# Transposing B, C and y of the last two batches with VectorE and a trip through DRAM instead of TensorE, with the second part of the work order rewritten

## The chip, the cores and the metric

The kernel runs on one core of one Trainium2 chip. The metric is the device time of one execution in microseconds (us), as the median of several runs. Five engines work side by side on the core and wait for one another through semaphores: TensorE (PE in the profile; its weight loads have a row of their own, PEld), VectorE (DVE), ScalarE (ACT), GpSimd (POOL) and SyncE (SP). Each engine takes its instructions strictly in the order in which they were written. In this kernel every DMA is issued by SP.

## The reference

Two blocks follow one another. The first is a state-space scan (Mamba2 in chunks), the second a token mixer of low rank followed by a two-layer network on the channels.

```python
# x (4, 8, 768, 32), a (4, 8, 768), B and C (4, 8, 768, 16): batch, head, step, size
for c in range(seq // 32):                      # per batch and head
    cum = cumsum(log(clip(a_c)))
    L = exp(cum[:, None] - cum[None, :]) * causal
    y_intra = ((C_c @ B_c.T) * L) @ x_c
    y_inter = (C_c @ state) * exp(cum)[:, None]
    y_c = y_intra + y_inter
    state = exp(sum(la)) * state + sum_j(B_j x_j * exp(cum[-1] - cum_j))
x = y.transpose(0, 2, 1, 3).reshape(4, 768, 256)        # heads side by side
h = x.transpose(0, 2, 1) @ U @ V                        # U (768, 32), V (32, 768)
u = x + h.transpose(0, 2, 1)
out = u + relu(u @ w_ch1) @ w_ch2                       # 256 -> 1024 -> 256
```

All inputs and the output are float32 (the weights of the second block come as float64 and are taken apart on the chip).

## The kernel before

**The scan** works on pairs of 128-step blocks. There are 4 batches with 3 pairs each, so pairs 0 to 11; pairs 6 to 8 belong to batch 2 and pairs 9 to 11 to batch 3. The steps of one pair are small functions. `load` brings B, C and x from DRAM. `prep` multiplies B and C by their decays into a tile BC (VectorE, one instruction of 128x512 elements). `turning` transposes the four 128x128 blocks of BC on TensorE into PSUM, from where ScalarE copies them to the tile T and writes two scaled versions of the C half to the tile Cm. `gram` multiplies Cm and T (TensorE), `mask` applies causality (VectorE), `state` and `update` advance the state, `inter` and `intra` make y in PSUM, and `yout` (ScalarE) copies y to yT, a tile with the channels on the partitions. `ytokening` transposes a pair of yT blocks back on TensorE into PSUM and copies them to ytok, a tile with the steps on the partitions (mostly by ScalarE for batches 0 and 1, by VectorE for batches 2 and 3).

**The mixer** of a batch takes ytok of all three pairs. `project` (p) multiplies it by U in 24 instructions, eight for each pair, in the order of the pairs; its result is copied to pT by ScalarE. `mixed` (x) multiplies by V into four PSUM banks, `added` (a) adds the result to yT on VectorE in two halves of two additions each.

**The channel network** of a batch goes over three blocks of 256 steps. `split` (S) cuts the block into a near, a far and a combined part (one ScalarE and two VectorE instructions), so that float32 products can be made of three fast products. `first` (f, 8 matmuls), `second` (e, 4 matmuls and a ReLU on ScalarE) and `third` (h, two VectorE instructions of 128x512) make a quarter of the hidden layer; `piece` (d) makes four matmuls of the second weight matrix at a time, thirteen pieces to a block, the last of which transposes or writes out. For batches 1 and 2 and most of 3 the last piece is a VectorE transpose in 32x32 squares and four DMAs of 64 KB to the output (line 909). Blocks 0 and 1 of batch 0 are computed in plain float32 products (`plain`, U, and slower pieces).

**Order.** Nothing is scheduled by the compiler: the strings in PLANS list the steps as words, and every word emits its instructions at its place on all the engines that it uses. The letters are P prep, D decayed, T turned (TensorE transposes of one pair, half of them per word), g gram, m and M mask, s state, u update, i inter, n intra, y yout, t ytokens, L load, R refined (weights), and p x a S f e h d for the mixer and the network with a lag: `p-1` is the projection of batch 2 and `p-2` that of batch 3, while T3 to T8 and t3 to t8 are the words of pairs 6 to 11. The tiles of PSUM come in three tags: w with two banks, x and z with three banks each. `gram`, `intra` and `mixed` each take two banks of x and two of z; `first` and the pieces take one.

Lines that matter below: 497, 501 and 507 (`turning`: transposes, copy to T, writes to Cm), 714 and 728 (`ytokening`), 529 (`gram`), 684 (`intra`), 659 (`inter`), 748 (`project`), 760 (`mixed`), 791 (all products of the channel network), 195 (loads), 909 and 923 (outputs). VectorE instructions go through a helper and are all on line 169.

Of the kernel before, what the change touches and what calls it, by code (L numbers as in the profile page):

```python
# [14 lines left out]
WCOLS = 512  # L15
NWORDS = 12
PLAIN = 2
ROWS = 3
FOUR = 3

# [50 lines left out]
}  # L71


# [1 line left out]
def kernel(  # L75
# [410 lines left out]
    def turning(k, c=0, n=2, tag="w", engine=None, sooner=False):  # L486

        s = st[k]
        if c == 0:
            s["T"] = att.tile([P, 2, 2, P], FP32, tag="T", name="T", bufs=3)  # L490
            s["Cm"] = att.tile([P, 2, 2, P], FP32, tag="Cm", name="Cm", bufs=3)
        tp = bank(tag, 2, n, P)
        for i in range(2):
            for v in range(n):
                if i or v:
                    yield
                nc.tensor.transpose(out=tp[:, i, v],  # L497
                                    in_=s["BC"][:, i, c + v].rearrange("p h n -> p (h n)"),
                                    identity=ident)
        if sooner or not engine:  # L500
            nc.scalar.copy(out=s["T"][:, :, c:c + n], in_=tp)
        for i in range(2):
            if engine:
                engine.tensor_scalar(out=s["Cm"][:, i, c:c + n], in0=tp[:, 1],
                                     scalar1=slot[:, i, None], scalar2=None, op0=ALU.mult)
            else:
                nc.scalar.activation(s["Cm"][:, i, c:c + n], tp[:, 1], AF.Copy,
                                     scale=slot[:, i, None])
        if engine and not sooner:
            nc.scalar.copy(out=s["T"][:, :, c:c + n], in_=tp)  # L510
        yield

    def turn(*args):
# [457 lines left out]

    def turned(k):

        t = turns.setdefault(k, turning(k))
        for _ in range(2):
            next(t)

    def crossed(k):

# [2 lines left out]
    def ytokens_of(k, v):  # L982
# [3 lines left out]

    scans = dict(P=prep, D=decayed, T=turned, g=gram, s=state, m=lambda k: mask(k, (0, 1)),
                 M=lambda k: mask(k, (2, 3)), u=update, i=lambda k: inter(k, 0), n=intra,
                 j=crossed, y=yout, t=ytokens, L=load, Q=lambda k, c: prep(k, c, 1),
                 E=lambda k, c: decayed(k, c, 1), O=ytokens_of,  # L990
                 V=lambda k, c, v: turn(k, c, 1, "wx"[v // 2 % 2], vector if v % 2 else None, v > 3))
    whole = dict(c=convert, R=refined, A=lambda i: decays(every_batch, "w", [i]),
# [56 lines left out]
```

## Time and profile before

| | |
|---|---|
| median of 3 runs | 219.41 us (219.27 to 221.42) |
| the profiled execution | 219.55 us, of which 217.8 us from the first to the last instruction |
| mean granted TensorE clock | 0.992 |
| busy: PE, PEld, DVE, ACT | 205.9, 185.1, 168.3 and 125.0 us |
| instructions: PE, DVE, ACT | 3246, 349 and 287 |
| DMA by the kernel | 83,984 packets, 14.13 MB |

The table gives busy time per engine within the span. The times in the profile count from the first instruction. A group such as "PE w L714 x4" in the chain is four instructions of line 714 that write a tile with tag w: here the four transposes of one pair.

### The profile page before, as it was taken

How to read it: one execution, taken by the hardware profiler on the slowest of the kernel's cores; microseconds unless marked ns; L12 is line 12 of the kernel's file. 1: busy time of each engine (PE TensorE's matmuls, PEld its weight loads, DVE VectorE, ACT ScalarE, POOL GpSimd, SP SyncE). 2: the span in 40 equal slices, each digit the busy share in tenths (PEclk: the TensorE clock that was granted, in tenths of full speed). 3: DMA queues.
4: the chain of work that ended last, by engine and by line, in shares of the span. 5: the costliest groups of instructions: out<-in, count | busy, mean ns of one | idle time of the engine just before them, and what ended most of it. 6: DMA issues, size and time to landing. Idle time of an engine off the chain costs nothing.

```text
span 217.8 us, 7530 instructions
## 1 busy us (share of the span) xinstructions
PE 205.9 (95%) x3246; PEld 185.1 (85%) x3246; DVE 168.3 (77%) x349; ACT 125.0 (57%) x287; POOL 6.6 (3%) x22
## 2 busy tenths in 40 slices
PE   7778799999999999999999999979999999999994
PEld 5555586878879998999999988869999899999993
DVE  3398978998899998699858967847994597874871
ACT  3353749479969774368589513667563276635410
POOL 4132100000000000000000000000000000000000
PEclk9999969999999999999999999999999999999999
DMA  5996789986751017406600020330000000033234
GB/s 82 134 159 178 105 123 225 249 147 157 99 73 26 3 50 97 52 16 87 147 6 0 0 40 14 50 54 0 3 0 3 3 2 0 3 48 51 36 60 96
DMA packets 84016, 14.60 MB, mean 67 GB/s; under 512 B 80336, under 2 KB 82192, under 8 KB 83984
## 3 DMA queue, kind: packets, MB, share of 16 engines
q1 hardware_dynamic: 83984, 14.13, 37.0%
q8 instruction: 25, 0.41, 0.9%
q14 instruction: 7, 0.06, 0.1%
HBM read 10.98 MB, written 3.15 MB: 65 GB/s over the span
## 4 chain that ended last, share of the span: by engine, by line
PE 83%; DVE 6%; ACT 3%; SPq 2%; issue 2%; DMA 2%; POOL 1%; DVEq 0%
PE x L791 35%; PE z L791 28%; PE x L529 3%; SPq L195 2%; PE w L497 2%; PE w L748 2%; PE w L714 2%; DMA bc<-in_B_dram 2%; DVE words L169 2%; PE x L760 2%; PE x L684 1%; PE x L659 1%; PE w L564 1%; PE z L684 1%; DVE M L169 1%
## 5 line engine op out<-in xcount | busy, mean ns | idle before, releaser
L169 DVE SCALAR_TENSOR_TENSOR words<-words 128x512 fp32r<-128x512 f32 (+6 forms) x60 | 39.3, 667 | 4.3 <-PE x L791 1.4
L791 PE MATMUL x<-words,w 128*128 128x256 f32 x288 | 38.3, 280 | 0.0
L791 PEld LDWEIGHTS x<-words,w 128*128 128x128 f32 x288 | 34.9, 188 | 1.8 <-issue 1.7
L791 PE MATMUL z<-u,w 128*128 128x256 f32 x240 | 34.0, 280 | 1.3 <-issue 1.3
L791 PE MATMUL x<-u,w 128*128 128x256 f32 x240 | 34.0, 281 | 0.0
L791 PEld LDWEIGHTS z<-u,w 128*128 128x128 f32 x240 | 30.1, 188 | 1.6 <-issue 1.3
L791 PEld LDWEIGHTS x<-u,w 128*128 128x128 f32 x240 | 30.1, 188 | 0.6 <-issue 0.2
L796 ACT ACTIVATE z<-z 128x512 f32<-128x512 f32 (+1 forms) x24 | 13.9, 578 | 18.0 <-PE z L791 18.0
L796 ACT ACTIVATE x<-x 128x512 f32<-128x512 f32 (+1 forms) x27 | 15.4, 574 | 14.5 <-PE x L791 14.3
L169 DVE SCALAR_TENSOR_TENSOR words<-x,words 128x512 fp32r<-128x512 f32 x20 | 13.7, 685 | 10.7 <-ACT words L831 10.5
L791 PE MATMUL z<-words,w 128*128 128x256 f32 x144 | 19.3, 280 | 0.0
L791 PEld LDWEIGHTS z<-words,w 128*128 128x128 f32 x144 | 17.5, 188 | 0.4 <-issue 0.4
L831 ACT ACTIVATE words<-z 128x512 fp32r<-128x512 f32 x20 | 11.8, 601 | 6.1 <-PE x L791 4.3
L831 ACT ACTIVATE words<-x 128x512 fp32r<-128x512 f32 x20 | 11.8, 600 | 4.8 <-PE x L791 4.7
L169 DVE SCALAR_TENSOR_TENSOR words<-z,words 128x512 fp32r<-128x512 f32 x20 | 13.6, 679 | 1.2 <-ACT words L831 1.2
L169 DVE SCALAR_TENSOR_TENSOR S<-S,kept,w 128x64 f32<-128x64 f32 x40 | 11.2, 279 | 1.6
L169 DVE TENSOR_TENSOR BC<-bc,F 128x512 f32<-128x512 f32 (+2 forms) x18 | 8.9, 508 | 4.2 <-DMA bc<-in_B_dram 2.8
L169 DVE TENSOR_TENSOR M<-x,causal 128x256 int32<-128x256 int32 x24 | 9.0, 417 | 3.8 <-PE z L529 3.8
L169 DVE TENSOR_TENSOR yT<-x,yT 128x384 f32<-128x384 f32 (+1 forms) x15 | 9.2, 612 | 3.2 <-PE z L760 3.1
L596 ACT ACTIVATE Sm<-S,slot 128x128 f32<-128x128 f32 (+1 forms) x18 | 6.1, 386 | 9.1 <-DVE S L169 9.1
L529 PE MATMUL x<-Cm,T 32*64 32x128 f32 x192 | 9.4, 307 | 1.7 <-DVE Cm L169 1.7
L659 PE MATMUL z<-T,Sm 32*64 32x64 f32 x180 | 7.7, 239 | 2.1 <-DVE settled L169 2.0
(152 smaller groups left out, 377.5 us busy)
## 6 DMA issues: line engine op xcount, KB each, us to landing
words<-in_moe_w_ch_dram SPq DMA_DIRECT2D x7, 512.0 KB, 5.9
x<-in_x_dram SPq DMA_DIRECT2D x24, 128.0 KB, 3.9
out_dram<-o SPq DMA_DIRECT2D x32, 64.0 KB, 2.2
bc<-in_B_dram SPq DMA_DIRECT2D x24, 64.0 KB, 3.3
bc<-in_C_dram SPq DMA_DIRECT2D x12, 128.0 KB, 3.7
out_dram<-words SPq DMA_DIRECT2D x3, 256.0 KB, 3.2
words<-in_moe_w_ch_dram SPq DMA_DIRECT2D x2, 256.0 KB, 4.8
out_dram<-o SPq DMA_DIRECT2D x2, 128.0 KB, 1.8
```

The lines of the kernel that those rows point to most:

```text
L169: self.last = call(*args, **kwargs)
L195: op = nc.sync.dma_start(**kwargs)
L497: nc.tensor.transpose(out=tp[:, i, v], in_=s["BC"][:, i, c + v].rearrange("p h n -> p (h n)"), identity=ident)
L529: nc.tensor.matmul(out=g[r][cols, c], lhsT=s["T"][rows, 0, c, cols], rhs=s["Cm"][rows, :, :, ts(2 * c + p, Q)].rearrange("r v t i -> r v i ...
L596: nc.scalar.activation(s["Sm"][:, sl, v], s["S"][:, sl, ts(v, D)], AF.Copy, scale=slot[:, v, None])
L659: product = nc.tensor.matmul(out=y[r // 2][p][ts(v, H), c], lhsT=own[ts(r, Q)], rhs=s["T"][ts(r, Q), 1, :, ts(2 * c + p, Q)].rearrange("r ...
L684: product = nc.tensor.matmul(out=y[n][p][ts(v, Q), c], lhsT=x_sb[k][half, c, h], rhs=s["M"][half, h // 2, c, h % 2], start=fresh(k, n, p, ...
L714: nc.tensor.transpose(out=t[c][:, c, g], in_=yT[b][:, g, ts(2 * q + c, P)], identity=ident)
L748: nc.tensor.matmul(out=p[ts(n, H)], lhsT=UU[:, c].rearrange("p t r -> p (t r)"), rhs=ytok[b][:, c, ts(n, P)], start=(c == 0), stop=(c == N ...
L791: nc.tensor.matmul(out=t, lhsT=lhsT, rhs=rhs, start=start, stop=True, skip_group_check=True)
L796: nc.scalar.activation(t, t, AF.Copy, scale=1.0 + EPS)
L831: nc.scalar.activation(gs[j, i][0], t, AF.Relu, scale=NEAR)
```

## The change

For pairs 6 to 11 the two kinds of TensorE transposes are replaced. `squared` takes the place of `turning`: VectorE transposes BC in 32x32 squares into a weight tile that is no longer needed (four such tiles are used in turn), four DMAs of 64 KB send its four groups of 32 partitions to a buffer in DRAM in runs of 128 bytes, and one DMA brings the 256 KB back into T with 128 partitions outermost, in runs of 512 bytes. That last DMA waits until the four sends have landed. The two writes to Cm then read T instead of PSUM. `squaring` takes the place of `ytokening` in the same way, with two VectorE transposes of 128x256, four sends and one fetch into ytok. The word T (t) of such a pair now comes twice: the first time for the transpose and the sends, the second time for the fetch (and, with T, the writes to Cm). The words after the 179th, from the middle of the work of batch 0 on, are written in another order; apart from the six additional t words it holds the same words.

```diff
--- before.py
+++ after.py
@@ -15,6 +15,7 @@
 WCOLS = 512
 NWORDS = 12
 PLAIN = 2
+SQUARED = 6
 ROWS = 3
 FOUR = 3
 
@@ -44,30 +45,30 @@
         'U1.0.0 g0 U1.0.1 g1 m0 M0 c5 c4 m1 M1 c5 D1 s0 u0 U1.1.0 U1.1.1 U1.1.2 i0 n0 y0 c6 c6 '
         's1 c5 g2 c7 u1 R2 m2 c7 U1.1.3 M2 c8 c8 c7 U1.0.2 L4 U1.0.3 i1 n1 y1 c6 R1 R0 c8 R5 c9 '
         's2 c9 c9 n2 d1.0 L5 R6 u2 R0 d1.1 P3 S1.2 d1.0 R7 d1.0 i2 y2 R3 t1 R1 t0 R2 R5 d1.1 R4 '
-        'f1.2.0 D4 T3 T3 P4 R7 R6 t2 f1.2.1 R3 D3 d1.1 f1.2.2 d1.0 R4 e1.2.0 d1.1 h1.2.0 e1.2.1 '
-        'T4 f1.2.3 d1.0 T4 e1.2.2 e1.2.3 h1.2.1 P5 g3 p0 m3 M3 L6 d1.2 d1.2 d1.2 T5 L7 d1.2 L8 '
-        'T5 h1.2.2 x0 h1.2.3 d1.2 a0.0 d1.2 d1.2 a0.1 S0.0 d1.2 g4 m4 s3 f0.0.1 D5 M4 f0.0.0 '
-        'd1.2 d1.2 d1.2 e0.0.0 e0.0.1 u3 h0.0.0 f0.0.2 d1.2 h0.0.1 f0.0.3 e0.0.2 s4 u4 n3 h0.0.2 '
-        'i3 e0.0.3 h0.0.3 d1.1 D6 S0.1 d1.2 d0.0 d0.0 y3 d0.0 d0.0 d0.0 S0.2 d0.0 d0.0 d0.0 D7 '
-        'n4 s5 i4 d0.0 d0.0 g5 P7 y4 u5 P6 m5 M5 d0.0 d0.0 t3 D8 f0.2.1 f0.1.2 s6 n5 i5 y5 '
-        'e0.1.2 u6 f0.2.0 f0.1.0 f0.1.3 h0.1.2 T7 e0.2.0 h0.2.0 e0.2.1 e0.1.3 h0.2.1 P8 T7 '
-        'h0.1.3 f0.1.1 d0.2 f0.2.2 f0.2.3 e0.1.0 h0.1.0 e0.1.1 h0.1.1 e0.2.2 e0.2.3 h0.2.3 d0.1 '
-        'd0.1 T6 T6 d0.1 d0.1 d0.1 t4 h0.2.2 t5 d0.1 d0.1 d0.1 d0.2 d0.2 d0.2 d0.2 d0.0 g7 m7 '
-        'p-1 d0.2 d0.2 x-1 M7 a-1.0 a-1.1 s7 d0.2 u7 d0.1 d0.1 d0.1 g6 m6 d0.1 M6 d0.1 d0.2 d0.2 '
-        'd0.2 d0.2 d0.2 S-1.0 T8 T8 i6 n6 y6 s8 n7 S-1.1 i7 y7 f-1.0.2 f-1.0.3 g8 e-1.0.2 '
-        'e-1.0.3 m8 M8 f-1.1.0 f-1.0.1 h-1.0.3 h-1.0.2 f-1.0.0 f-1.1.1 e-1.1.0 e-1.0.0 e-1.0.1 '
-        'h-1.1.0 h-1.0.1 e-1.1.1 f-1.1.2 h-1.0.0 d-1.0 S-1.2 f-1.1.3 e-1.1.2 h-1.1.2 d-1.0 d-1.0 '
-        'd-1.0 d-1.0 f-1.2.0 u8 d-1.0 d-1.0 h-1.1.1 d-1.1 e-1.2.0 h-1.2.0 t6 e-1.1.3 f-1.2.2 '
-        'd-1.1 d-1.1 d-1.0 h-1.1.3 e-1.2.2 h-1.2.2 d-1.1 d-1.1 d-1.1 d-1.1 d-1.1 i8 n8 t7 d-1.1 '
-        'd-1.1 y8 d-1.1 t8 p-2 d-1.1 x-2 d-1.0 d-1.0 a-2.0 f-1.2.1 a-2.1 S-2.0 d-1.0 d-1.0 S-2.1 '
-        'f-1.2.3 e-1.2.1 h-1.2.1 f-2.0.2 e-1.2.3 f-2.0.0 f-2.0.1 d-1.2 d-1.2 e-2.0.0 h-1.2.3 '
-        'e-2.0.2 h-2.0.0 f-2.0.3 S-2.2 h-2.0.2 d-1.2 e-2.0.1 d-1.2 d-1.2 d-1.2 e-2.0.3 h-2.0.3 '
-        'f-2.1.0 h-2.0.1 f-2.1.1 f-2.1.2 e-2.1.0 e-2.1.1 h-2.1.0 f-2.1.3 d-1.2 d-1.2 d-1.1 '
-        'e-2.1.2 h-2.1.1 f-2.2.1 e-2.1.3 d-2.0 d-1.2 d-1.2 d-2.0 d-2.0 d-2.0 h-2.1.2 d-1.2 d-1.2 '
-        'd-2.1 d-2.1 d-1.0 h-2.1.3 f-2.2.0 f-2.2.2 d-2.0 d-2.0 d-2.0 d-2.0 e-2.2.2 d-2.1 e-2.2.0 '
-        'h-2.2.0 d-1.2 h-2.2.2 d-2.0 d-2.0 f-2.2.3 d-2.1 d-2.1 d-2.1 e-2.2.3 d-2.0 d-2.1 d-2.1 '
-        'e-2.2.1 h-2.2.3 d-2.0 d-2.2 d-2.2 d-2.2 d-2.0 h-2.2.1 d-2.1 d-2.1 d-2.1 d-2.1 d-2.2 '
-        'd-2.1 d-2.2 d-2.2 d-2.2 d-2.2 d-2.2 d-2.2 d-2.2 d-2.2 d-2.2 '),
+        'P4 f1.2.1 T3 f1.2.2 f1.2.0 d1.1 R3 e1.2.0 e1.2.2 f1.2.3 T4 e1.2.1 R7 T3 t2 R4 T4 h1.2.0 '
+        'L6 h1.2.1 P5 d1.1 T5 d1.0 h1.2.2 e1.2.3 p0 g3 m3 M3 d1.0 d1.2 d1.2 d1.2 d1.2 d1.1 R6 D3 '
+        'x0 h1.2.3 d1.2 d1.2 d1.2 d1.2 s3 a0.0 g4 a0.1 m4 d1.2 d1.2 S0.0 d1.2 f0.0.0 u3 d1.2 '
+        'f0.0.1 e0.0.0 f0.0.2 e0.0.1 T5 n3 L7 e0.0.2 d1.2 f0.0.3 M4 D4 s4 i3 h0.0.0 y3 e0.0.3 '
+        'h0.0.1 d0.0 D5 n4 s5 h0.0.2 u4 i4 P6 L8 y4 d0.0 d0.0 D6 t3 h0.0.3 S0.1 d0.0 S0.2 d0.0 '
+        'T6 d0.0 d0.0 d0.0 g5 m5 M5 u5 d0.0 d0.0 d0.0 d0.0 f0.1.2 P8 P7 f0.1.3 T7 n5 s6 i5 y5 t5 '
+        'e0.1.2 e0.1.3 f0.1.0 D7 f0.1.1 t3 f0.2.0 h0.1.2 e0.1.0 e0.1.1 u6 f0.2.2 h0.1.3 f0.2.1 '
+        'f0.2.3 h0.1.1 e0.2.2 h0.1.0 e0.2.0 d0.1 e0.2.1 h0.2.0 e0.2.3 T7 d0.1 T6 d0.1 d0.2 d0.2 '
+        'd0.1 d0.1 t4 h0.2.2 d0.1 d0.1 h0.2.1 d0.1 d0.0 h0.2.3 D8 T8 d0.2 d0.2 d0.2 s7 u7 g6 m6 '
+        'd0.2 d0.2 d0.2 d0.1 d0.1 d0.1 d0.1 d0.2 M6 d0.2 d0.2 d0.2 s8 u8 i6 n6 y6 t4 t5 p-1 T8 '
+        'd0.1 d0.2 g7 x-1 m7 M7 a-1.0 a-1.1 n7 S-1.0 i7 g8 y7 m8 M8 S-1.1 f-1.0.2 f-1.0.1 n8 i8 '
+        'y8 e-1.0.2 t7 t6 h-1.0.2 t8 f-1.1.0 f-1.0.0 f-1.1.1 e-1.1.0 h-1.1.0 f-1.0.3 e-1.0.0 '
+        'e-1.1.1 h-1.1.1 e-1.0.1 h-1.0.1 f-1.1.2 e-1.0.3 h-1.0.3 f-1.1.3 h-1.0.0 d-1.0 S-1.2 t7 '
+        'd-1.0 e-1.1.2 e-1.1.3 d-1.0 d-1.0 d-1.1 d-1.1 h-1.1.3 d-1.0 d-1.0 d-1.0 d-1.0 d-1.1 '
+        'f-1.2.0 t6 d-1.0 d-1.0 d-1.0 d-1.0 h-1.1.2 t8 p-2 d-1.1 x-2 a-2.0 e-1.2.0 a-2.1 d-1.1 '
+        'd-1.1 d-1.1 S-2.0 f-1.2.1 d-1.1 f-1.2.2 e-1.2.1 f-2.0.2 f-1.2.3 h-1.2.0 h-1.2.1 e-1.2.2 '
+        'h-1.2.2 f-2.0.3 e-2.0.2 h-2.0.2 e-1.2.3 h-1.2.3 d-1.0 f-2.0.0 d-1.2 S-2.1 d-1.2 d-1.2 '
+        'd-1.1 d-1.1 d-1.1 d-1.1 f-2.0.1 e-2.0.0 f-2.1.2 e-2.0.1 h-2.0.0 e-2.0.3 d-1.1 d-1.2 '
+        'd-1.2 e-2.1.2 h-2.0.1 h-2.1.2 d-1.2 d-1.2 h-2.0.3 S-2.2 f-2.1.0 d-1.2 f-2.1.1 e-2.1.0 '
+        'h-2.1.0 d-2.0 d-2.0 d-2.0 d-2.0 d-2.0 d-2.0 f-2.1.3 d-1.2 d-1.2 d-1.2 d-1.2 e-2.1.3 '
+        'e-2.1.1 h-2.1.1 f-2.2.0 f-2.2.2 d-2.1 d-1.2 f-2.2.1 d-2.1 d-2.1 h-2.1.3 e-2.2.0 d-2.0 '
+        'd-2.0 e-2.2.1 h-2.2.1 e-2.2.2 d-2.1 f-2.2.3 d-2.0 h-2.2.2 d-2.0 d-2.0 d-2.0 e-2.2.3 '
+        'd-2.1 d-2.1 d-2.1 d-2.1 h-2.2.0 d-2.2 d-2.2 d-2.2 d-2.1 d-2.0 h-2.2.3 d-2.1 d-2.1 d-2.1 '
+        'd-2.2 d-2.2 d-2.1 d-2.2 d-2.2 d-2.2 d-2.2 d-2.2 d-2.2 d-2.2 d-2.2 '),
 }
 
 
@@ -508,6 +509,60 @@
                                      scale=slot[:, i, None])
         if engine and not sooner:
             nc.scalar.copy(out=s["T"][:, :, c:c + n], in_=tp)
+        yield
+
+    turns_by = {}
+
+    def squares(key):
+
+        n = len(turns_by)
+        turns_by[key] = n
+        t = w1f[n % NQ].rearrange("p c m -> p (c m)")
+        d = nc.dram_tensor(f"squares{n}", [16, Q, 4, Q], FP32, kind="Internal").ap()
+        return t, d
+
+    def send(sq, d):
+
+        return [nc.sync.dma_start(
+            out=d[:, :, r].rearrange("w x t -> x w t"),
+            in_=sq[ts(r, Q)].rearrange("x (w t) -> x w t", t=Q)) for r in range(4)]
+
+    def fetch(dst, d, sent):
+
+        op = nc.sync.dma_start(out=dst, in_=d.rearrange("(w g) x a t -> (g x) w (a t)", w=4))
+        for s in sent:
+            hold(op, s)
+
+    def squared(k):
+
+        s = st[k]
+        s["T"] = att.tile([P, 2, 2, P], FP32, tag="T", name="T", bufs=3)
+        s["Cm"] = att.tile([P, 2, 2, P], FP32, tag="Cm", name="Cm", bufs=3)
+        sq, d = squares(("T", k))
+        vector.transpose(
+            out=sq.rearrange("p (w g t) -> p w g t", g=4, w=4),
+            in_=s["BC"].rearrange("p i c h n -> p (i c) (h n)").rearrange(
+                "p w (g t) -> p w g t", g=4))
+        sent = send(sq, d)
+        yield
+        yield
+        fetch(s["T"].rearrange("p i c t -> p (i c) t"), d, sent)
+        for i in range(2):
+            nc.scalar.activation(s["Cm"][:, i], s["T"][:, 1], AF.Copy, scale=slot[:, i, None])
+        yield
+        yield
+
+    def squaring(k):
+
+        b, q = pairs[k]
+        sq, d = squares(("y", k))
+        for n in range(NCB):
+            vector.transpose(
+                out=sq.rearrange("p (c n e x) -> p n c e x", e=4, c=2, n=2)[:, n],
+                in_=yT[b][:, n, ts(q, 2 * P)].rearrange("p (c e x) -> p c e x", c=2, e=4))
+        sent = send(sq, d)
+        yield
+        fetch(ytok[b][:, 2 * q:2 * q + 2].rearrange("p c (n t) -> p (c n) t", t=P), d, sent)
         yield
 
     def turn(*args):
@@ -971,9 +1026,18 @@
 
     def turned(k):
 
-        t = turns.setdefault(k, turning(k))
+        t = turns.setdefault(k, (squared if k >= SQUARED else turning)(k))
         for _ in range(2):
             next(t)
+
+    sides = {}
+
+    def sided(k):
+
+        if k < SQUARED:
+            ytokens(k)
+        else:
+            next(sides.setdefault(k, squaring(k)))
 
     def crossed(k):
 
@@ -986,7 +1050,7 @@
 
     scans = dict(P=prep, D=decayed, T=turned, g=gram, s=state, m=lambda k: mask(k, (0, 1)),
                  M=lambda k: mask(k, (2, 3)), u=update, i=lambda k: inter(k, 0), n=intra,
-                 j=crossed, y=yout, t=ytokens, L=load, Q=lambda k, c: prep(k, c, 1),
+                 j=crossed, y=yout, t=sided, L=load, Q=lambda k, c: prep(k, c, 1),
                  E=lambda k, c: decayed(k, c, 1), O=ytokens_of,
                  V=lambda k, c, v: turn(k, c, 1, "wx"[v // 2 % 2], vector if v % 2 else None, v > 3))
     whole = dict(c=convert, R=refined, A=lambda i: decays(every_batch, "w", [i]),
```

## The prediction

> **What bounds the kernel now.** I read the page first: busy times, slices, the chain, the queues.
>
> ```profile
> PE 205.9 (95%) x3246; PEld 185.1 (85%) x3246; DVE 168.3 (77%) x349; ACT 125.0 (57%) x287; POOL 6.6 (3%) x22
> ...
> PE   7778799999999999999999999979999999999994
> ...
> DMA  5996789986751017406600020330000000033234
> ...
> q8 instruction: 25, 0.41, 0.9%
> ...
> PE 83%; DVE 6%; ACT 3%; SPq 2%; issue 2%; DMA 2%; POOL 1%; DVEq 0%
> ```
>
> PE is busy 95% of the span and is 83% of the chain that ended last. DMA is nearly idle in the second half. The busy times by stage, for the stretch in which the order changes, and the chain there:
>
> ```profile
> 60.00:88.00 28.00, 27.84 (x314) 24.30 (x313) 26.47 (x48) 20.08 (x44) 0.00 (x0) 1.00 0.34 51
> 88.00:115.00 27.00, 27.00 (x609) 25.63 (x588) 20.49 (x47) 17.37 (x46) 0.00 (x0) 1.00 0.34 60
> 115.00:145.00 30.00, 28.65 (x543) 25.96 (x542) 22.69 (x43) 15.86 (x40) 0.00 (x0) 1.00 0.17 27
> 145.00:170.00 25.00, 25.00 (x314) 24.35 (x315) 18.61 (x32) 14.01 (x30) 0.00 (x0) 1.00 0.02 4
> 170.00:200.00 30.00, 30.00 (x265) 29.32 (x264) 22.19 (x35) 15.31 (x29) 0.00 (x0) 1.00 0.10 16
> ```
> ```profile
> 106.49 0.44 PE w L714 x4
> ...
> 121.56 0.44 PE w L497 x4
> ...
> 123.38 0.87 PE w L714 x8
> ...
> 142.07 1.26 issue
> ...
> 191.44 3.63 PE x L791 x32
> ...
> 214.64 0.42 DVE o L169
> ```
>
> The columns after the stretch and its length are busy time of PE, PEld, DVE, ACT and POOL, clock, DMA share and GB/s. From 60 us to 214.6 us, where the last matmul ends, PE waits for almost nothing; the largest hole is 1.26 us of "issue". Any PE work taken out there shortens the run, and any wait put in lengthens it. DVE at 26.5 of 28 us between 60 and 88 is the second thing to watch. One network matmul costs 3.63 / 32 = 0.113 us, so f is 0.91 and e and a piece of d 0.45.
>
> **The change part by part.** *Removed from PE:* four transposes for B and C and four for y, for six pairs: twelve groups of four. The rows give 0.44 us a group (0.87 for two). 12 x 0.44 = 5.3 us, all on the path.
>
> *Moved to DVE, taken from ACT:*
>
> ```profile
> L169 DVE STREAM_TRANSPOSE o<-yT 128x512 f32<-128x512 f32 x8 | 5.6, 705 | 0.1
> ...
> L169 DVE COPY ytok<-w 128x512 f32<-128x512 f32 x6 | 4.1, 685 | 3.1 <-PE w L714 3.1
> ...
> L507 ACT ACTIVATE Cm<-w,slot 128x256 f32<-128x256 f32 x18 | 7.7, 490 | 0.0
> ...
> L501 ACT COPY T<-w 128x512 f32<-128x512 f32 x9 | 5.3, 592 | 4.7 <-PE w L497 4.5
> ```
>
> Six 128x512 squares at 0.705 are 4.2 us. A 128x256 square has no row; it lies between 0.35 (half) and 0.705, I take 0.43, near the 0.42 of the other 128x256 instructions: twelve are 5.2. Six copies of 0.685 go (4.1). Net DVE +5.3 us, to 173.6, still under PE, so at nothing, except where a chain through DVE gates PE (below). ACT loses six copies of 0.592. The writes to Cm from SBUF instead of PSUM stay at 0.49; the copy of twice the size at 0.592 bounds them above. Both are hidden under PE's work.
>
> *Added on SP:* 60 DMAs. Nearest are the outputs, which also write 32 partitions in runs of 128 bytes:
>
> ```profile
> 127.24 2.75 SPq L909 DMA_DIRECT2D out_dram<-o  x4
> ...
> 137.56 6.71 SPq L909 DMA_DIRECT2D out_dram<-o  x8
> ```
> ```profile
> words<-in_moe_w_ch_dram SPq DMA_DIRECT2D x2, 256.0 KB, 4.8
> ...
> out_dram<-words SPq DMA_DIRECT2D x3, 256.0 KB, 3.2
> ...
> out_dram<-o SPq DMA_DIRECT2D x32, 64.0 KB, 2.2
> out_dram<-o SPq DMA_DIRECT2D x2, 128.0 KB, 1.8
> ```
>
> Four sends take 2.75 us to issue, and the last lands 2.2 after its issue begins, about 4.3 after the first. The fetch has no row: 256 KB lands in 3.2 (a write) or 4.8 us (a load beside much traffic), 128 KB with 128 partitions in 1.8. I take 3.2, the row of the same size in a quiet queue, with 1.8 and 4.8 as ends. One trip is then 0.7 + 4.3 + 3.2 + 0.9 (two writes to Cm) = 9.1 us instead of 1.5 to 2 us. [...]
>
> *Where a trip is waited for.* SP issues in the written order. I laid out the words of the new order with these durations. Most trips have 10 us or more of PE work between the sends and the use (pairs 8 to 11 and the y of batch 3), so they are hidden: if that cover went, each would cost up to its 9 us. Two places have less.
>
> *First place, T3 and T4 (pairs 6 and 7).* The row of DVE and PE where the orders part:
>
> ```profile
> 66.56 1.29 PE L791 MATMUL x<-u,w 128*128 128x256 f32 x8
> ...
> 79.41 0.35 PE L529 MATMUL x<-Cm,T 32*64 32x128 f32 x2
> ```
> ```profile
> 68.76 0.42 DVE L169 TENSOR_TENSOR bd<-bc,FD 128x256 f32<-128x256 f32 x1
> 69.10 0.69 DVE L169 TENSOR_TENSOR BC<-bc,F 128x512 f32<-128x512 f32 x1
> 69.70 0.69 DVE L169 TENSOR_TENSOR words<-o,w 128x512 f32<-128x512 f32 x1
> 70.42 0.69 DVE L169 SCALAR_TENSOR_TENSOR w<-words,w 128x512 fp32r<-128x512 f32 x1
> ```
>
> PE begins its first reordered word at 66.56 in the old order and the gram of pair 6 at 79.41. By durations 11.85 us of PE work lie between (4 f, 4 e, three float32 pieces of 1.55, 12 transposes), so 1.0 us is waiting. In the new order it is 12.0 us: the eight transposes of T3 and T4 are out, project p0 is in. DVE is at 68.76 there. P4 comes next, the square of T3 ends at 70.1. Its sends issue until 72.85. The square of T4 follows two refining instructions (1.4 us) and is done by 72.2, so T4's four sends stand in SP's queue ahead of T3's fetch, which issues at 75.6 and lands at 78.8. Cm is written by 79.65. ACT has waited for that with the copy of ytok (t2) queued behind, and after it T4's Cm, a ReLU and pT: t2's copy ends at 80.25, the last third of p0 (0.5 us) waits for it, and gram starts at 80.75. Without waits it would be 66.56 + 12.0 = 78.56. So 2.2 us of waiting instead of 1.0: **+1.2 us** (with the ends of the fetch: 0 to +2.8).
>
> *Second place, p-1.* The second t4 and t5 stand directly ahead of p-1, and between the sends of t4 and these fetches SP has four outputs and the four sends of T8: 3 x 2.75 = 8.25 us of issue. T8's square stands behind seven `third`s (1.37 each) that DVE works off meanwhile, and comes about 3.4 us behind PE's place. t5's fetch then lands about 0.4 us after p-1 needs it: **+0.4** (0 to 3 with the ends).
>
> *After p-1* the old order had much batch-1 work to fill in; the new order has used it up:
>
> ```profile
> 130.77 0.52 PE x L760 x2
> ...
> 140.72 1.12 PE x L791 x8
> ```
> ```profile
> 102.03 0.38 PE x L684 x32
> 102.42 0.40 PE z L684 x21
> ```
> ```profile
> L169 DVE TENSOR_TENSOR M<-x,causal 128x256 int32<-128x256 int32 x24 | 9.0, 417 | 3.8 <-PE z L529 3.8
> ...
> L169 DVE TENSOR_TENSOR yT<-x,yT 128x384 f32<-128x384 f32 x8 | 4.4, 553 | 3.1 <-PE z L760 3.1
> ```
>
> Between x-1 and the first f of batch 2 lay 9 us of PE work; now it is n7, i7 and g8, about 2.0 us (0.8 for an intra by the second pair of rows, less for each of the others). The chain through DVE is the mask of g7 (four of 0.417, overlapping to 1.5), four additions (0.553 each, 2.1 overlapping) and the far part (0.65); the mixer holds its four PSUM banks until those additions, so that n7 waits too, and g8 and the first f wait for banks that y7's copies on ACT free. Counted step by step the first f starts 5.8 us after p-1 ends, where g7, x-1 and the three words are 3.6 to 3.7: **+2.1 us** (0.8 if the banks come free sooner, 3.5 if ACT is late with y7 as well).
>
> *The rest of the reordering* I cost at nothing: PE order has the same words, all ready with room. Ends: -1.3 (the "issue" hole goes, since the dense scan words are spread more) and +1.5.
>
> **The sum**: 219.55 - 5.3 + 1.2 + 0.4 + 2.1 = 217.95. The profiled run stands 0.14 above the median of 219.41, so 217.8 us.
>
> **The rivals.**
>
> *All trips hidden.* If fetches land in 1.8 us and the banks turn over sooner, the waits go: 219.4 - 5.3 = 214.1. For it: 9 us of slack in most trips, DMA idle. Against: T3's fetch behind T4's sends is written in SP's order.
>
> *The trip becomes the bound, slower.* Place: the two places above. Rows:
>
> ```profile
> q8 instruction: 1, 0.02, 5.2%
> ...
> out_dram<-o SPq DMA_DIRECT2D x2, 64.0 KB, 4.1
> ```
>
> Two blocks of outputs in a row already took 6.71 us instead of 5.5, with landings of 4.1 us, in the 2 us in which a 16 KB load of instructions ran. With sends at 4.1 (+1.9) and fetches at 4.8 (+1.6) each place is 3.5 later: 217.8 + 7 = 224.8. It decides (over 1% slower) from 3.8 us in all, about 1.9 at each place. [...]
>
> *Code loading is slowed.* The 1.26 us hole falls just behind that same load. If 60 DMAs make PE pay it six times among its 25 loads: 217.8 + 7.6 = 225.4. [...]
>
> *It doesn't do what it says:* if PE's transposes had filled waits, nothing would be saved: 219.4. The chain's own rows speak against it.
>
> **How the numbers follow.** Forecast 0.42, all hidden 0.27, trip as the bound 0.19, code loading 0.06, nothing saved 0.06. One per cent (2.2 us, 217.2 to 221.6) is about what a measurement tells from no change. Of the forecast 0.12 falls below 217.2 and 0.02 above 221.6; of the slower two 0.05 and 0.02 stay within. Faster 0.12 + 0.27 = 0.39; slower 0.02 + 0.14 + 0.04 = 0.20, which I raise to 0.23 for waits in the last 60 us that I have not priced; same 0.38. The range takes in all hidden with a little of the "issue" hole, 213.7, and reaches into the slower ones to 222.6.
>
> **What would show it.** PE's busy time down by the transposes, no transposes of pairs 6 to 11 on it. ACT waiting some 4 us for a DMA into T near 75; PE waiting near p0, at p-1 and ahead of the first f of batch 2. The prediction is wrong if those holes are absent (faster) or if fetches land after 5 us and holes at PE exceed 8 us in all (slower).

## The result and the profile after

The changed kernel is faster by 0.2 to 1%, depending on which executions are counted. The ratio of its time to that of the kernel before, from executions that lay side by side, is 0.9898 with an interval of 0.9862 to 0.9934. Measured once more in another series, the same code gave 0.9933 (0.9888 to 0.9978). The median of all its 21 executions is 219.67 us against 220.14 for 21 of the kernel before in the same series, a ratio of 0.998 (0.995 by the means). The two ratios above, and all those below, take only executions within 1.5% of the fastest of the same kernel, 9 of 21 and 7 of 11 of the changed one, and the granted clock of those left out (0.982 to 1.00) is that of those kept (0.983 to 1.00). The profiled execution took 219.02 us, 0.53 less than that of before.

The page of the changed kernel, its busy times, slices, queues, chain and DMA landings:

```profile
PE 204.6 (94%) x3198; PEld 182.3 (84%) x3198; DVE 172.1 (79%) x361; ACT 122.2 (56%) x281; POOL 6.6 (3%) x22
...
PE   7788879999999998999999999899999999999994
...
PEclk9969979999999999999999999999999999999999
DMA  6994879888544449445755546634630003302034
...
q8 instruction: 25, 0.41, 0.9%
...
PE 71%; DVE 8%; DMA 6%; SPq 5%; ACT 5%; issue 3%; DVEq 0%; ACTq 0%
...
squares<-w1f SPq DMA_DIRECT2D x48, 64.0 KB, 2.0
T<-squares SPq DMA_DIRECT2D x6, 256.0 KB, 3.5
ytok<-squares SPq DMA_DIRECT2D x6, 256.0 KB, 3.5
```

PE has 48 matmuls fewer, the twelve groups of four. DVE has 3.8 us more (5.3 were forecast) and ACT 2.8 us less (six copies of 0.592, or 3.6, were to go). The row PEclk has two dips in the first fifth where the kernel before has one (`PEclk9999969999` there); they lie ahead of the first word whose place changed, in code that is the same. So spans are not compared below, but **the stretch** from the first word whose place changed to the last matmul. Its start and end in the changed kernel, from the timeline and the chain:

```profile
68.09 0.58 PE L846 MATMUL z<-u,w 128*128 128x256 f32 x2
```
```profile
214.17 0.42 DVE o L170
```

That is 146.08 us, against 66.56 to 214.64 or 148.08 before: 2.0 us less, where the prediction's terms make 1.6. In the second profile of the same code the stretch is 145.07 us (67.43 to 212.50), so one profile is good to about 1 us. The old order has a second profile too, with traffic added that nobody waits for (below): 147.80 us. All in all the stretch is 1.7 to 3.0 us shorter. The 1.5 us between the two starts (68.09 and 66.56) are a difference of the head alone, and it nearly hid the gain in the profiled times.

The stages that the prediction read, in the changed kernel (columns as there):

```profile
60.00:88.00 28.00, 26.72 (x242) 22.90 (x240) 26.08 (x46) 18.68 (x41) 0.00 (x0) 1.00 0.61 101
88.00:115.00 27.00, 26.82 (x626) 24.54 (x625) 23.61 (x53) 16.38 (x44) 0.00 (x0) 1.00 0.53 93
115.00:145.00 30.00, 29.30 (x538) 26.37 (x537) 25.22 (x55) 16.75 (x43) 0.00 (x0) 1.00 0.55 113
145.00:170.00 25.00, 25.00 (x314) 23.70 (x313) 18.99 (x34) 13.29 (x28) 0.00 (x0) 1.00 0.32 66
```

PE now waits 1.3 us between 60 and 88 where it waited 0.2, and the share of DMA has grown from 0.34 to 0.61 there.

**First place.** The timeline of the changed kernel around T3 and T4:

```profile
70.90 0.70 DVE L170 STREAM_TRANSPOSE w1f<-BC 128x512 f32<-128x512 f32 x1
...
71.64 5.95 SPq L526 DMA_DIRECT2D squares<-w1f  x8
...
72.83 0.70 DVE L170 STREAM_TRANSPOSE w1f<-BC 128x512 f32<-128x512 f32 x1
...
77.77 1.76 SPq L532 DMA_DIRECT2D T<-squares  x2
...
80.72 0.91 ACT L551 ACTIVATE Cm<-T,slot 128x256 f32<-128x256 f32 x2 [3.62 <-DMA T<-squares]
...
81.54 0.57 ACT L783 COPY ytok<-w 128x512 f32<-128x512 f32 x1
...
82.16 0.66 PE L803 MATMUL w<-ytok,UU 128*64 128x128 f32 x8 [0.82 <-ACT ytok L783]
...
82.75 0.35 PE L584 MATMUL x<-Cm,T 32*64 32x128 f32 x2
```

This is the chain as forecast: eight sends in one block (5.95 us), T3's fetch behind them, ACT 3.62 us idle ahead of Cm, the copy of ytok behind Cm, the last third of p0 behind the copy, and then the gram of pair 6. It starts 14.66 us after 68.09, where the prediction counted 12.0 us of PE work: 2.7 us more in place of the old 1.0, so +1.7 where +1.2 was forecast. Other profiles of the same words give less: in the second profile of the changed kernel the eight sends took 4.43 us, PE waited 0.20 us for the copy, and the gram started 14.02 us after the beginning, so +1.0; in the kernel with y6 moved (below) it was 4.39 us and 13.86, so +0.9.

**After p-1.** The timeline of the changed kernel there:

```profile
136.43 1.53 PE L803 MATMUL w<-ytok,UU 128*64 128x128 f32 x24
136.43 1.30 DVE L170 STREAM_TRANSPOSE o<-yT 128x512 f32<-128x512 f32 x2
...
137.82 0.27 ACT L761 COPY yT<-x 128x128 f32<-128x128 f32 x1 [0.63 <-DVE o L170]
...
139.37 0.27 ACT L808 COPY pT<-w 128x128 f32<-128x128 f32 x1
139.69 0.19 PEld L815 LDWEIGHTS x<-V,pT 32*128 32x128 f32 x2 [0.90 <-ACT pT L808]
...
143.81 1.21 PE L846 MATMUL x<-u,w 128*128 128x256 f32 x8
```

p-1 has no wait for a DMA; it ends at 137.96. The first f of batch 2 starts 5.85 us later (forecast 5.8; 5.4 in the second profile).

### The profile page after: what moved, and what is told of

It reads as the page before. It is cut to its first block, busy times and chain, and to the rows that moved or that the text cites. A ratio compares the mean times of both kernels' runs of the same rounds, so it can differ in the third digit from the quotient of the medians.

```text
span 217.3 us, 7514 instructions
## 1 busy us (share of the span) xinstructions
PE 204.6 (94%) x3198; PEld 182.3 (84%) x3198; DVE 172.1 (79%) x361; ACT 122.2 (56%) x281; POOL 6.6 (3%) x22
## 4 chain that ended last, share of the span: by engine, by line
PE 71%; DVE 8%; DMA 6%; SPq 5%; ACT 5%; issue 3%; DVEq 0%; ACTq 0%
PE x L846 32%; PE z L846 24%; DMA bc<-in_B_dram 4%; SPq L196 4%; DVE words L170 2%; PE x L584 2%; ACT yT L759 2%; PE x L815 2%; PE x L739 2%; SPq L526 1%; DMA T<-squares 1%; PE z L739 1%; PE x L803 1%; DVE BC L170 1%; PE w L619 1%
## 5 line engine op out<-in xcount | busy, mean ns | idle before, releaser
L846 PE MATMUL x<-words,w 128*128 128x256 f32 x288 | 37.2, 279 | 0.0
L846 PE MATMUL x<-u,w 128*128 128x256 f32 x240 | 33.4, 281 | 0.0
L584 PE MATMUL x<-Cm,T 32*64 32x128 f32 x192 | 10.5, 309 | 1.4 <-DVE Cm L170 1.3
```

The source lines that it names most:

```text
L584: nc.tensor.matmul(out=g[r][cols, c], lhsT=s["T"][rows, 0, c, cols], rhs=s["Cm"][rows, :, :, ts(2 * c + p, Q)].rearrange("r v t i -> r v i ...
L846: nc.tensor.matmul(out=t, lhsT=lhsT, rhs=rhs, start=start, stop=True, skip_group_check=True)
```

## The experiments

All the kernels compute the whole output. The theory under test was the prediction's sum: TensorE's transposes are 5.3 us on the path, and waits of the new trips and of the new order give about 3.7 back. The rivals: the order alone does something, the traffic itself costs time, or the waits come from other causes than named.

**The order without the squares, and each half of the squares.** Three kernels in the new order; all or some pairs from 6 on keep TensorE's transposes, at the first of the two words. As the transposes need the PSUM banks w, a few words had to move.

```diff
-        t = turns.setdefault(k, (squared if k >= SQUARED else turning)(k))
+        if k >= SQUARED and PE_T:
+            if k not in turns:
+                turns[k] = turn(k)
+            return
...
-        if k < SQUARED:
-            ytokens(k)
+        if k < SQUARED or PE_Y:
+            if k not in sides:
+                sides[k] = ytokens(k)
```

> The new order with TensorE transposes for all pairs, done at the first T and t word of a pair (T6 and t3 moved behind u5, t5 behind u6, where the PSUM banks of tag w are free). Theory (the gain comes from the 48 transposes, the new order by itself costs the waits around x-1): 5.3 us of PE work come back, the wait at p0 of 0.8 to 1.7 us goes, a little is lost on the w banks: the stretch from the first reordered word to the last matmul 149.5 to 151.5 us against 146.1 of the changed kernel and 148.1 of the one before, so 220.5 to 223 us. Rival (the new order is the gain): 217 us or less.

> The new order, B and C by squares, y by TensorE (t3 moved behind u5, t5 behind u6). Theory: 2.64 us of PE work come back and the y trips cost nothing now, so the stretch is 148.5 to 149.5 us and the time 2.0 to 3.0 us above the changed kernel. Rival (the y trips gate p-1): the stretch stays at 146 to 147.

> The new order, y by squares, B and C by TensorE (T6 moved behind u5). Theory: 2.64 us of PE work come back, the wait at p0 (0.8 us, with gram 1.7) goes, so the stretch is 146.8 to 148 us, about 1 us above the changed kernel. Rival (B and C trips are as well hidden as those of y): 148.7 us, as in the run with T squared only.

Measured: order alone 1.0466 (1.0381 to 1.0551) of the time before, stretch 158.5 us; squares for B and C alone 1.0302 (1.0233 to 1.0371), stretch 153.05; squares for y alone 1.0385 (1.0305 to 1.0465), stretch 156.35. All three are well above what was expected, and above their rivals. What PE waits for in the order alone, and in B and C alone, in the stretch (the sum, the times and the longest):

```profile
PE w L771 <- DVE S L172: 2.3, 1, 2.3
PE w L500 <- DVE BC L172: 1.8, 2, 1.5
```
```profile
PE w L770 <- DVE S L171: 3.2, 1, 3.2
```

TensorE's transposes wait for their input BC and for a bank w that VectorE's update of the state (S) still reads; the squares need no bank, and no wait of PE in the changed kernel has a row that names them. The order alone is 12.4 us longer than the changed kernel (158.5 against 146.1). Of that 5.3 are the transposes by their rows, 4.1 these waits (all waits of PE in the stretch are 6.1 us against 1.9 in the changed kernel), and 1.7 a 3.4 us window at half clock that begins at 110; 1.3 stay unassigned. So the new order, with the transposes at these words, has no room for them, and it isn't the order by itself that gains. The price of each half can't be read from these runs, since waits that my placing made are in them.

**The squares in the old order.** The old order with the squares, and the fetches of y ahead of p-1 and p-2; two loads moved back.

```diff
-        'p-1 d0.2 d0.2 x-1 M7 a-1.0 a-1.1 s7 d0.2 u7
+        't3 t4 t5 p-1 d0.2 d0.2 x-1 M7 a-1.0 a-1.1 s7 d0.2 u7
...
-        y8 d-1.1 t8 p-2
+        y8 d-1.1 t8 t6 t7 t8 p-2
```

> The squares and their trips, but the words in the old order (each fetch of y stands ahead of the projection that needs it; the loads of pairs 10 and 11 are two words later, after n3 and i4, since SP would otherwise stand still). Theory (the trips cost 9 us each and only the new order hides them): the two T words of a pair stand together there, so ScalarE waits out most of a trip for each of six pairs, and PE soon after; 5.3 us saved against some 4 us lost at four to six places, so 232 to 245 us. Rival (the order matters little, trips are hidden by the slack that is there anyway): 213 to 218 us.

Measured: 1.2445 (1.2363 to 1.2527), 273.06 us; more than the 232 to 245 expected. The waits of this kernel:

```profile
ACT Cm L551 <- DMA T<-squares: 49.3, 6, 14.5
...
PE w L803 <- DMA ytok<-squares: 17.4, 2, 11.0
```

Without distance between send and use ACT stands 49.3 us in front of the six fetches, up to 14.5 at a time, more than a trip of 9, which fits sends that stand behind an earlier fetch in SP's queue (argued, not measured by itself). The mean clock fell to 0.893. Without a reordering the squares are no use here.

**The traffic alone.** The kernel before, with 48 sends and 11 fetches of the same sizes and forms added at its own T and t words, into tiles that nobody reads.

> The kernel before, with all the sends and fetches of the change added where the T and t words of pairs 6 to 11 stand (from weight tiles no longer needed, back into one of them; nothing uses the result). Theory (traffic by itself is free; a trip costs only where it is waited for): within 0.7 us of the kernel before, stretch 147.6 to 149. Rival (DMA traffic slows the loading of instructions or the other engines): PE holes of over 1 us named issue, 221.5 to 227 us.

Measured: 0.9998 (0.9966 to 1.0029), stretch 147.80 us against 148.08 before. Between 60 and 115 us, by stages:

```profile
60.00:88.00 28.00, 27.83 (x256) 24.50 (x255) 26.42 (x47) 20.59 (x46) 0.00 (x0) 1.00 0.48 78
88.00:115.00 27.00, 27.00 (x637) 25.27 (x636) 21.53 (x49) 16.80 (x46) 0.00 (x0) 1.00 0.63 110
```

PE is as busy as before beside a DMA share of 0.48 and 0.63 (0.34 before), and there is still just one hole of "issue", of 1.0 us. Here the transfers cost nothing where nobody waits for them; the rival by which code loading is slowed falls with that.

**T3's fetch ahead of T4's sends.** The words of T3, T4 and t2 changed round, and the writes to Cm made a third T word, for pair 6 behind the copy of ytok. T8's fetch also comes ahead of p-1.

```diff
-  ... f1.2.3 T4 e1.2.1 R7 T3 t2 R4 T4 h1.2.0 L6 h1.2.1 P5 d1.1 T5 d1.0 h1.2.2 e1.2.3 p0 g3
+  ... f1.2.3 e1.2.1 R7 t2 T3 T4 R4 h1.2.0 T4 L6 h1.2.1 P5 d1.1 T5 d1.0 h1.2.2 e1.2.3 T3 p0 g3
...
         fetch(s["T"].rearrange("p i c t -> p (i c) t"), d, sent)
+        yield
+        yield
         for i in range(2):
```

> The changed kernel with T3's fetch ahead of T4's sends, the copy of ytok (t2) ahead of it, and the writes to Cm as a third T word of their own, placed shortly before the gram that needs them. Theory (the first wait is T3's fetch behind T4's four sends with the ytok copy behind it on ScalarE): p0 waits for nothing, the gram of pair 6 starts 12.0 to 13.0 us after the first reordered word instead of 14.7, and the stretch to the last matmul is 144.3 to 145.3 us instead of 146.1. Rival (the time is given back at the next wait, or VectorE gates the gram anyway): gram at 14 us or more, stretch 145.8 to 146.5.

Measured: 0.997 (0.9926 to 1.0014) of before, stretch 146.56. The timeline of this kernel:

```profile
66.74 0.58 PE L848 MATMUL z<-u,w 128*128 128x256 f32 x2
...
79.81 0.61 PE L805 MATMUL w<-ytok,UU 128*64 128x128 f32 x8
...
80.50 0.35 PE L586 MATMUL x<-Cm,T 32*64 32x128 f32 x2
```

The gram of pair 6 starts 13.76 us after the stretch begins instead of 14.66, and p0 waits for nothing. So the link named for the first place is there, and without it PE's wait of 0.82 us is gone. How much it costs is less sure: the unaltered words gave 14.02 and 13.86 in two other profiles, so that the edit is worth 0.1 to 0.9 us at this gram, and the 12.0 to 13.0 expected were not reached. But the gram of pair 7 then waits 1.09 us for its own Cm, whose writes stand behind T4's later fetch, and it starts 21.83 us after the beginning against 21.6 (20.9 in the second profile). The gain is given back at the next pair, as the rival had it; the stretch, 146.56, lies at the rival's upper end (145.8 to 146.5).

A further version moved T4's writes to Cm up as well:

```diff
-  x0 h1.2.3 d1.2 d1.2 d1.2 d1.2 s3 a0.0 T4 g4
+  x0 h1.2.3 T4 d1.2 d1.2 d1.2 d1.2 s3 a0.0 g4
```

> fetch_first with T4's writes to Cm ahead of the next channel pieces instead of behind them. Theory (fetch_first won 1 us at gram 6 and lost it at gram 7, whose Cm stood on ScalarE behind a piece that PE had not made yet): gram 7 starts 20.3 to 20.9 us after the first reordered word (21.8 in fetch_first, 21.6 in the changed kernel), the stretch is 144.3 to 145.5 us and the ratio 0.98 to 0.99. Rival (the y fetches ahead of p-1 take it back in their turn): gram 7 early, but stretch 145.8 to 146.6, ratio 0.99 to 1.0.

Measured: 0.9911 (0.9862 to 0.996), the same as the changed kernel. The gram of pair 7 starts 20.67 after the beginning, and the first f of batch 2 after 75.1 (75.8 in the changed kernel, 74.85 in its second profile). The stretch is 147.76, above what was expected (144.3 to 145.5) and above the rival. From that f to the last matmul it took 2.4 us longer than both, with no wait. The chains of this kernel and of the changed one show why, by the same 32 matmuls:

```profile
182.31 3.77 PE x L848 x32
```
```profile
183.26 3.63 PE x L846 x32
```

Each matmul took 0.118 us instead of 0.113, from 142 us to the end, at a granted clock of 1.00. That is no property of the version. It is told below.

**y6 behind p-1**, as the banks that y6 empties, and its place on ACT ahead of pT, could hold up x-1.

```diff
-  s8 u8 i6 n6 y6 t4 t5 p-1 T8
+  s8 u8 i6 n6 t4 t5 p-1 y6 T8
```

> The changed kernel with the word y6 behind p-1, so that the copy of p-1's result stands ahead of y6 on ScalarE. Theory (x-1 waits 1.4 us because its input's copy stands behind y6, and y6 waits for VectorE to write out the last blocks of batch 1): x-1 starts 0.5 to 1 us sooner after p-1, stretch 145.2 to 145.7. Rival (the banks that y6 holds gate x-1 as well): no change, 146.1.

Measured: 0.9971 (0.9929 to 1.0013), stretch 146.13 against 146.08 (145.07 in the second profile): no change clear of the spread. pT is now copied right behind p-1, but in this kernel's chain the gram of pair 10 then waits for y6's copies to empty its banks, and x-1 stands behind the gram. That is the rival. x-1 starts 1.4 us after p-1 ends; it was 1.7 and 1.2 us in the two profiles of the changed kernel.

**p-1 far earlier.** T and t words of batch 2 earlier, p-1 and x-1 ahead of the last pieces of batch 1, and, in one of two kernels, the first work of batch 2 drawn up as filling.

```diff
-  D8 T8 d0.2 d0.2 d0.2 s7 u7 g6 m6 ... s8 u8 i6 n6 y6 t4 t5 p-1 T8 d0.1 d0.2 g7 x-1
+  D8 T8 d0.2 d0.2 d0.2 p-1 s7 u7 g6 m6 M6 d0.2 d0.2 d0.2 d0.1 d0.1 d0.1 d0.1 x-1 ... s8 u8
```

> The changed kernel with the fetch of T3 ahead of T4's sends and Cm as a third word (as in fetch_first, T4's Cm now ahead of the channel pieces), and with the y of pairs 7 and 8 fetched early, so that p-1, x-1, the additions and S-1.0 stand ahead of the last pieces of batch 1, and f-1.0.2, f-1.0.1 and e-1.0.2 fill in around the gram of pair 10. Theory (the change loses 1 to 1.7 us at p0 and gram 6, and some 2 us between p-1 and the first f of batch 2, since that chain has nothing beside it): both go at least in part, stretch 142.5 to 145 us, ratio 0.965 to 0.98. Rival (PSUM banks and VectorE hold the chain wherever it stands, and what is won at one wait is lost at the next): stretch 145.5 to 147.

> As early_p, but with the gram of pair 10 ahead of f-1.0.1 and with e-1.0.2 and h-1.0.2 left where they were. Theory: within 0.7 us of early_p, since only the filling around gram differs. Rival (the order of those few words decides): over 1 us apart.

Measured: 1.0107 (1.0058 to 1.0156) with the filling and 1.0102 (1.0049 to 1.0156) without. In the first the stretch is 149.8, 3.7 above the changed kernel, where 142.5 to 145 was expected. Its waits and the ten microseconds in question:

```profile
ACT yT L763 <- PE z L716: 5.1, 6, 3.2
...
PE x L848 <- ACT u L842: 1.5, 1, 1.5
```
```profile
135.00:145.00 10.00, 8.20 (x261) 6.58 (x254) 5.94 (x14) 5.61 (x15) 0.00 (x0) 0.83 0.36 57
```

Now PE waits 1.5 us for ScalarE's u, and a window at half clock falls into this stage: 0.83 over 10 us is 3.4 us at a half, worth 1.7. In the second version the stretch is 152.5, with 10.2 us at half clock; by their medians the two lie 0.2 us apart. The place after p-1 was not made cheaper by moving it; whether a better filling exists stays open.

**Every fetch twice.** Each fetch is followed by a second one of the same data, which waits for the first.

```diff
         for s in sent:
             hold(op, s)
+        again = nc.sync.dma_start(out=dst, in_=...)
+        hold(again, op)
```

> The changed kernel with every fetch made twice, the second after the first has landed: each trip is 3.5 to 4 us longer. Theory (only T3 and T4 at the first place and t4, t5, T8 near p-1 have no slack): 3.5 us at the first place, 3.5 to 7 us near p-1, none elsewhere: 224 to 229 us. Rival (all twelve trips are on the path): 42 us more, 255 us or above. Rival (all hidden): 217 to 218.

Measured: 1.0861 (1.0802 to 1.0921), stretch 165.94, 19.9 us more where the expectation's terms make 7 to 10.5. The waits of this kernel in the stretch:

```profile
ACT Cm L554 <- DMA T<-squares: 18.2, 5, 5.5
...
PE w L806 <- DMA ytok<-squares: 6.4, 3, 3.1
...
PE x L587 <- ACT Cm L554: 4.7, 1, 4.7
```
```profile
80.00:90.00 10.00, 7.39 (x77) 5.89 (x78) 5.96 (x13) 5.05 (x11) 0.00 (x0) 0.83 0.95 159
130.00:145.00 15.00, 10.30 (x175) 9.38 (x181) 5.71 (x15) 3.49 (x8) 0.00 (x0) 0.77 0.57 120
175.00:190.00 15.00, 11.31 (x87) 9.24 (x87) 6.61 (x11) 2.74 (x6) 0.00 (x0) 0.77 0.20 54
```

Some 3 us more of latency for each of twelve fetches (they land in 3.1 us median here) made ACT wait at five of the six T fetches (at two in the changed kernel) and PE at three fetches of ytok, two of them for p-2. The edit does more than lengthen a trip: the second fetch waits at SP for the first, up to 3.4 us at a time, and what stands behind it in SP's order is issued later. The three stages have 3.4, 6.9 and 6.9 us at half clock (twice 0.17 of 10 us, twice 0.23 of 15), which cost at most half of that, 8.6 us. At least 11.3 us are left without it, a little above what was expected.

**The changed kernel again**, for the run-to-run spread beside the early versions.

> The changed kernel unaltered, beside the two below on the same chip. By its profile the stretch from the first reordered word to the last matmul is 146.1 us against 148.1 before; with the head equal on average, a ratio of 0.985 to 0.995.

Measured: 0.9933 (0.9888 to 0.9978). Its timeline at p-1:

```profile
134.75 1.21 PE L803 MATMUL w<-ytok,UU 128*64 128x128 f32 x16
136.15 0.66 PE L803 MATMUL w<-ytok,UU 128*64 128x128 f32 x8 [0.19 <-DMA ytok<-squares]
```

Here the last fetch of y does come late, by 0.19 us.

## Why the prediction was right, point by point

The direction, the places and roughly the size were right: 0.9927 (217.8 over 219.41) was forecast, 0.9898 and 0.9933 were measured, and 0.998 by the medians of all executions. The two likeliest cases, faster by over 1% (0.39) and within 1% (0.38), meet at this result. That the stretch shrank by 2.0 to 3.0 us where the terms make 1.6 is in part luck: the hole of 1.3 us that the sum had left standing went, and in the first profile other losses took back most of it, while in the second the three places cost 0.7 us less than forecast. In absolute terms 219.67 lies 1.9 us above 217.8; the kernel before, too, measured 0.7 above its first median in the same series (220.14 against 219.41), and what makes up the other 1.2 is not shown.

- **-5.3 us for twelve groups of transposes, all on the path.** Held as far as the stretch can say: 5.3 saved, 1.7 and 2.2 us of waiting added at two places and the hole of 1.3 us of "issue" gone make 2.7, against 2.0 measured. In the second profile, with 1.0, 0.2 and 1.8 us added at the three places, they make 3.6, against 3.0. So 0.6 to 0.7 us of loss remain in either and have no row. The order alone, with the transposes back, is longer by them and by waits that have rows.
- **VectorE +5.3 us, ScalarE less, both hidden.** The squares took 0.705 and 0.421 us (0.705 and 0.43 forecast). Busy DVE rose by 3.8 instead of 5.3. No wait of PE names the added instructions.
- **The trip, 9.1 us.** The fetch lands in 3.5 us median (2.9 to 5.5 for T, 3.2 to 4.3 for y) where 3.2 was taken, within the ends 1.8 and 4.8 but for one; sends in 2.0 against 2.2.
- **First place, +1.2.** The mechanism was right link by link; +1.7, +1.0 and +0.9 in three profiles, so the size was right within the spread. The squares stood where they were laid out (70.90 is 2.81 us into the stretch, 2.84 forecast). In the first profile the eight sends took 5.95 us in one block instead of 5.5, so that T3's fetch was issued 0.6 us later than laid out, and the gram followed 0.5 later; in the two others they took 4.4. One reading was wrong: the "1.0 us of waiting" in the old order is no waiting. PE was busy for all of the 12.85 us there, since between other words an f cost 1.0 to 1.1 us and an e 0.55 to 0.67, not 0.91 and 0.45 (and the 11.85 us of the prediction contain 16 transposes, not 12). As many f and e stand in the new order, so the error falls out of the difference. The rows of such an f and an e in the kernel before, each with the start of the next word:

```profile
71.05 1.29 PE L791 MATMUL x<-u,w 128*128 128x256 f32 x8
72.18 1.89 PE L791 MATMUL x<-words,o 128*128 128x256 f32 x8
73.72 0.82 PE L791 MATMUL x<-u,w 128*128 128x256 f32 x4
74.38 1.89 PE L791 MATMUL z<-words,o 128*128 128x256 f32 x8
```

  What the prediction did not see is a wait of 0.29 us right at the beginning of the new order, for weights that ScalarE copies.

- **Second place, +0.4.** In the changed kernel 0 and in its second profile 0.19: mis-sized within its bounds, and the smallest term.
- **After p-1, +2.1.** 5.85 us (5.4 in the second profile) against 5.8, but by a somewhat different chain. The step that I missed: y6's copies on ACT wait 0.63 us for the last VectorE transposes of batch 1 to leave the yT buffer, and pT stands behind them. Moving pT ahead of them changed nothing clear of the spread, as the gram of pair 10 waits for the same copies.
- **The rest at 0, with -1.3 as an end for the "issue" hole.** This step failed: the hole is gone, and -1.3 was the right value. Against it stands the remainder of 0.7 us, about 0.5 of which may be the slower pace of matmuls between 113 and 127 us in that profile: 2.35 us for 20 in the first fence (the changed kernel), 1.81 for 16 in the second (before).

```profile
121.53 2.35 PE z L846 x20
```
```profile
125.63 1.81 PE x L791 x16
```

- **"Most trips have 10 us or more of PE work between the sends and the use".** Too generous, by what the doubled fetches suggest: with some 3 us more for a fetch (and a later SP), five of the six trips of B and C and three of the six of y came after their first reader. It made no error in the sum, but the rival "the trip becomes the bound" may have been nearer than its 0.19 said. It did not come, as fetches took 3.5 and not 4.8 us and sends 2.0 and not 4.1.
- **All trips hidden** (214.1) fell at the first place, **code loading** with the traffic alone, **nothing saved** with the stretch.

## What to carry to other kernels

Moving transposes from a saturated engine to one with room and a trip through DRAM paid here, by 1% at best, and only with an order of work that leaves a trip's latency between send and use (in the old order the same squares took 1.2445 of the time). Count that distance on the issuing queue and not only on the engine that uses the data: in the changed kernel T3's fetch was issued behind eight sends that took 5.95 us, and with every fetch made twice SP waited up to 3.4 us at a time, with the next sends behind it. Where two kernels share a long head, compare the stretch behind the first difference, and take more than one profile: the head alone varied by 1.8 us here (starts of the stretch from 66.34 to 68.16), about as much as the gain.

## What was not expected of the hardware

**Half-clock windows follow waits of PE.** In the profiles of the kernel before and of the changed one the granted clock is 1 or 0.5, and up to the last matmul each window at 0.5 lasts 3.41 us (from 28.53 on before; from 12.29 and from 29.36 on after). In other kernels the mean clocks fit 3.4 us or a multiple of it: 0.83 of 10 us in the first early version, 0.77 of 15 us twice in the doubled fetches, 10.2 us in the second early version (0.977 of 221.9). Within the stretch there is none in the kernel before and in the changed one. There is one each in the order alone, in the squares for y alone and in the first early version, at waits of PE of 2.3, 2.2 and 1.5 us, and there are more in the second early version, in the doubled fetches and in the old order with squares (mean clock 0.893). In the one of the squares for y alone 16 matmuls of the channel network took 3.40 us, 0.21 each instead of 0.113. Not every hole brings one: the squares for B and C alone have a wait of 3.2 us, and the 24 matmuls of the network that follow its four transposes took 2.74 us, 0.114 each. Before the stretch there are none, one or two, by the execution, in the same code, and the stretch starts at 66.34 us in the profile with none, at 66.56 to 66.78 with one and at 67.43 to 68.16 with two. PE need not be idle for all of the time ahead of a window: in the 3.41 us right ahead of one it was busy for 2.03 us in the kernel before (25.11 to 28.53), and for 1.57 and 0.98 us in the changed one (8.88 to 12.29 and 25.94 to 29.36). Nor does that amount settle it: in the kernel before PE was busy for 1.75 us from 8.05 to 11.46 and for 2.15 from 141.17 to 144.58, around the hole of "issue", and no window came behind either. What sets one off is not shown. In the first early version the window of 3.4 us cost up to 1.7 us more than the wait ahead of it, an estimate from half its length.

**A second, slower pace at full granted clock.** Some profiles have long phases in which the network matmuls take 0.118 us instead of 0.113, by the rows of 32 above (3.77 and 3.63 us) 3.9% more, at a granted clock of 1.00: from 142 us to the end in the second fetch version (2.4 us lost), from 150 on in the squares for y alone, from 113 to 127 in the changed kernel. It is not tied to a version: from 113 us on the changed kernel took 0.118 in one profile (16 in 1.89 us) and 0.113 in the other (12 in 1.36 us). No view says what sets it. On that account alone one profile of this kernel can be 1.1% off (2.4 of 219.2 us).

**Sends and fetches beside a busy core were free in this kernel:** 59 DMAs and about 6 MB more at 0.9998 (0.9966 to 1.0029).
